# Earlier narrow rows, a new order of tap transfers and edge zeros on another engine, in a fused forward and backward kernel of an attention block

## The chip, the cores and the metric

One core of one Trainium2 chip. The metric is the device time in microseconds (us), median of several executions. A ratio of two kernels is the mean time of one kernel's fast runs over that of the other's fast runs of the same rounds, so it is not quite the ratio of the medians quoted.

PE is TensorE, DVE is VectorE, ACT is ScalarE, POOL is GpSimd, SP issues DMAs.

## The reference

```python
# B, T, D, K = 2, 4000, 144, 5; bf16
xa = layernorm(x)
q, k, v = split(xa @ w_qkv, 3)
glob = softmax(q @ k.T / sqrt(D)) @ v @ w_att_out
u, g = split(gelu(layernorm(x) @ w_mlp_in), 2)
loc  = (u * conv5(layernorm(g), dw_csgu)) @ w_mlp_out
m    = concat(glob, loc)
out  = x + (m + conv5(m, dw_merge)) @ w_merge
# returned: out, and for grad_out the gradients of
# x, w_qkv, w_att_out, w_mlp_in, dw_csgu, w_mlp_out, dw_merge, w_merge
```

## The kernel before

It does one batch after the other. Each batch has a head (transposes and projections of x and of grad_out), an attention (forward and backward, 32 blocks of rows, with the gated convolution worked off in its gaps) and a tail (gradients of the projections). D is 144, so every operand comes as 128 columns and a narrow rest of 16.

The head makes `goT`, the transposed gradient with two columns of zeros at each edge. The zeros are set by POOL. The projections of the gradient (`pb`) read this tile, the first of them with the left edge.

```python
def phase_head(k, W, b, S, nrm, ld, wts):
    ...
    goT = S.Pall[:, 2 * GW:3 * GW + 4]
    nc.gpsimd.memset(goT[:, 0:2], 0.0)
    nc.gpsimd.memset(goT[:, 2 + TT_:], 0.0)
    ...
    def stB(n, tile_q, tile_w, tile_d):
        ...
            for m in range(5):
                nc.tensor.matmul(pb[:], goT[:, i * 128 + m:i * 128 + m + 128], W.GL[...], ...)
```

The narrow rest of the keys, 16 rows, is spread by DMA to four groups of partitions, so that narrow matmuls can use it. `R_d` is a saved copy of the same rows. These DMAs go through one queue, in this order, once the head has all rows:

```python
    def spread():
        nc.sync.dma_start(S.R_d[:], R[112:128, :])
        for p in range(2):
            nc.sync.dma_start(S.Rz[p][112:128, :], ...)
        for q in range(2):
            for r in (2 * q, 2 * q + 1):
                for c0, c1, x in S.XRw:
                    nc.sync.dma_start(x[32 * r:32 * r + DR, :, 0:SC], ...)
```

The convolutions keep neighbour taps: `put` stores a block's edge rows to memory, `fill` loads the rows around a block. The tails do the same with a `fill` of their own, and POOL packs gradient taps to 80 rows (`rows80`, seen in the profile as `g<-gs`) for PE's `EF` matmuls. In the first tail POOL also computes the norm for the second batch.

Of the kernel before, what the change touches and what calls it, by code (L numbers as in the profile page):

```python
# [15 lines left out]
DR = 16  # L16
# [1043 lines left out]
TT_ = 4000  # L1060
NGR = 8
LASTR = TT_ - 31 * 128
GW_ = [512] * 7 + [416]
SC = 500
# [380 lines left out]
def phase_head(k, W, b, S, nrm, ld, wts):  # L1445

    nc, tc = k.nc, k.tc
    with ExitStack() as es:
# [4 lines left out]
        GW = NBK * 128  # L1453
        R = S.Sm[:, 2, :]
        goT = S.Pall[:, 2 * GW:3 * GW + 4]
        nc.gpsimd.memset(goT[:, 0:2], 0.0)
        nc.gpsimd.memset(goT[:, 2 + TT_:], 0.0)
        go80 = {}
        first = S.ab.tile([128, 16, 128], BF, tag="ST", bufs=3, name="go80f")
        late = S.ab.tile([128, 16, 128], BF, tag="PT", bufs=3, name="go80l")  # L1460
# [26 lines left out]
        def stT(g):  # L1487
            pm = ps_t.tile([128, 4, 128], BF, tag="tp")
            for j in range(4):
                nc.tensor.transpose(pm[:, j, :], S.xaa[:, g * 4 + j, 0:128], id_[:])  # L1490
            nc.scalar.copy(S.xaT[:, g * 512:(g + 1) * 512], pm[:].rearrange("p a b -> p (a b)"))
            pr = ps_t.tile([128, 4, 128], BF, tag="tp")
            for j in range(4):
                nc.tensor.transpose(pr[:, j, :], S.xaa[:, g * 4 + j, 16:D], id_[:])
            (nc.scalar.copy if b == 0 and g % 2 else nc.vector.tensor_copy)(R[:, g * 512:(g + 1) * 512], pr[:].rearrange("p a b -> p (a b)"))
# [30 lines left out]
                    put_dug.pop()()  # L1526

        def spread():
            nc.sync.dma_start(S.R_d[:], R[112:128, :])
            for p in range(2):  # L1530
                nc.sync.dma_start(S.Rz[p][112:128, :], R[112:128, p * 256:(p + 1) * 256])
            for q in range(2):
                for r in (2 * q, 2 * q + 1):
                    for c0, c1, x in S.XRw:
                        nc.sync.dma_start(x[32 * r:32 * r + DR, :, 0:SC], R[112:128, 0:TT_].rearrange("p (a h c) -> p a h c", h=2, c=SC)[:, c0:c1, q, :])

        def jit0():
            S.jt0 = [S.xp.tile([128, 4, 128], BF, tag=t_, name=t_) for t_ in ("QTm", "BTm", "QBr")]
# [13 lines left out]
        with tc.manual_schedule():  # L1552
            rest = None
            for g in range(3):
                if g not in S.gs:
                    take_go(k, S, b, g, ld)
            if wts:
                wts.heads(ps_t, ps_2, lambda: nrm.stats(0))
                nrm.power(0)
                wts.taps1(0)  # L1560
                wts.keys(ps_t, ps_2)
                nrm.shift(0)
                narrow(0)
                nrm.apply(0)
                wts.taps()
                wts.taps1(1)
                nrm.stats(1)
                nrm.power(1)
                stA(0)
                take_go(k, S, b, 3, ld)  # L1570
                stT(0)
                wts.rows(ps_2, 0)
                nrm.shift(1)
                nrm.apply(1)
                narrow(1)
                nrm.stats(2)
                nrm.power(2)
                wts.rows(ps_2, 1)
                rest = wts.rest(ps_t, ps_2)
            else:  # L1580
                narrow(0)
                narrow(1)
                stA(0)
                take_go(k, S, b, 3, ld)
                stT(0)
            for n in range(-1, NGR):
                if 1 <= n + 2 < NGR:
                    stT(n + 2)
                if n == 3:
                    jit0()  # L1590
                if n >= 0:
                    stB(n, *tiles())
                if 1 <= n + 2 < NGR:
                    stA(n + 2)
                if wts and n + 3 < NGR:
                    nrm.shift(n + 3)
                    nrm.apply(n + 3)
                if n + 3 < NGR:
                    narrow(n + 3)
                if wts and n + 4 < NGR:  # L1600
                    nrm.stats(n + 4)
                    nrm.power(n + 4)
                if n + 5 < NGR and n + 5 not in S.gs:
                    take_go(k, S, b, n + 5, ld)
                for f in put_dug[:len(put_dug) - n % 2]:
                    f()
                del put_dug[:len(put_dug) - n % 2]
                if n == 5:
                    spread()
                if n == 4:  # L1610
                    jit()
                if rest:
                    next(rest, None)
            for _ in rest or ():
                pass
            for f in put_dug:
                f()
            del put_dug[:]
# [153 lines left out]
def local_steps(k, W, b, S, es, ps, Q):  # L1772

    nc, tc = k.nc, k.tc
# [18 lines left out]
    def pair(p):  # L1793
        def aft(*keys):

            return tuple(((n, p - d), 0) for n, d in keys if p >= d)
# [55 lines left out]
        gn = wk.tile([128, 2, D], BF, tag="gn_t", bufs=6, name="gn_t")  # L1852
        for j in range(2):
            nc.scalar.activation(gn[:, j, :], h_[:, j, D:2 * D], ACT.Identity, bias=nm[:, j:j + 1], scale=rs[:, j:j + 1])
        yield 'P', 2, aft(("gn", 1), ("ug", 2), ("wg", 4))
        gnC.put(p, gn)
        Q.mark("gn", p)
        dug = wk.tile([128, 2, D], BF, tag="dug", name="dug")
        nc.sync.dma_start(dug[:], S.dug_d[:, 2 * p:2 * p + 2, :])
        yield 'V', 4  # L1860
        gnC.fill(p)
        yield 'P', 4, ((("gn", min(p + 1, NPR - 1)), 10),) + aft(("ug", 1))
        pc = gnC.conv(p, False)
        gc = wk.tile([128, 2, D], BF, tag="gc", bufs=1, name="gc")
# [10 lines left out]
        nc.vector.tensor_tensor(dh[:, :, 0:D], du[:], gp[:, :, 0:D], op=ALU.mult)  # L1875
        nc.sync.dma_start(S.ug_d[:, 2 * p:2 * p + 2, :], ug[:])
        Q.mark("ug", p)
        yield 'P', 1, aft(("dg", 1), ("dh", 3), ("wg", 4))
        dgC.put(p, dgc)
        Q.mark("dg", p)  # L1880
        yield 'V', 4
        dgC.fill(p)
        yield 'P', 4, ((("dg", min(p + 1, NPR - 1)), 10),) + aft(("dh", 1))
        s12 = sm.tile([128, 2, 2], F32, tag="s12", name="s12")
        dg = wk.tile([128, 2, D], BF, tag="dgf", bufs=1, name="dgf")
# [223 lines left out]
def phase_tail(k, W, b, S, nrm, nxt):  # L2109
# [3 lines left out]
    with ExitStack() as es:  # L2113
# [60 lines left out]
        def fill(g):  # L2174
            for h in range(2):
                r_ = G["r", h, g] = wk.tile([128, 512], BF, tag="r80_%d" % h, name="r80")
                taps[h].load(r_[0:80, :], g * 512, 512, nc.scalar)
# [121 lines left out]
        with tc.manual_schedule():  # L2299
            loads(0)  # L2300
            load_dh(0)
            load_dh(1)
            loads(1)
            rows80(0)
            prep(0)
            for h in range(NPR + 5):
                g, hf = divmod(h, 2)
                if 0 < h < NPR:
                    turn_dx2(*turn_dx(h))
                if hf == 0 and 0 <= g - 2 < NGR:  # L2310
                    fill(g - 2)
                if hf == 0 and g < NGR:
                    turn(g, 0)
                    corr(g, 0)
                    turn(g, 1)
                    corr(g, 1)
                elif g < NGR:
                    if g:
                        corr(g, 2)
                    corr(g, 3)  # L2320
                if h == 0:
                    turn_dx2(*turn_dx(0))
                    corr(0, 2)
                if 0 <= h - 1 < NPR:
                    sums_act(h - 1)
                    sums_dve(h - 1)
                if hf == 0 and g < NGR:
                    put(g)
                if nrm:
                    for lag, f_ in ((5, nrm.apply), (4, nrm.shift), (3, nrm.power), (2, nrm.stats), (1, nrm.load)):  # L2330
                        q, m = divmod(h - lag, 2)
                        if m == 0 and 0 <= q < NGR:
                            f_(q)
                    if NPR + 2 <= h < NPR + 4:
                        narrow_go(k, nxt, h - NPR - 2, nrm.ld)
                if h == NPR - 1:
                    spill_ef()
                if fin_ and 4 <= h < NPR - 1:
                    fin_.loads(h - 4)
                if g + 1 < NGR:  # L2340
                    (rows80 if hf else prep)(g + 1)
                if 0 <= h - 1 < NPR:
                    means(h - 1)
                if 0 <= h - 2 < NPR:
                    fin(h - 2)
                if h == NPR + 4:
                    spill_gr()
                if 0 <= h - 5 < NPR:
                    out_mm(h - 5)
                if fin_ and h == NPR + 4:  # L2350
                    fin_.gr_out()
                if NPR <= h < NPR + 4:
                    for q in range(4):
                        j = (h - NPR) * 8 + 2 * q
                        gr_part(range(j, j + 2))
                        if fin_:
                            fin_.step((h - NPR) * 4 + q)
                if h < NPR:
                    dx_mm(h)
                if hf == 0 and 0 <= g - 1 < NGR:  # L2360
                    load_x(g - 1)
                if nrm and NPR - 2 <= h < NPR + 1:
                    take_go(k, nxt, 1, h - NPR + 2, nrm.ld)
                if hf == 1 and g + 2 < NGR:
                    load_dh(g + 2)
                    loads(g + 2)
# [346 lines left out]
```

## Time and profile before

| | before |
|---|---|
| time, median of 3 (lowest to highest) | 1281.05 us (1277.03 to 1282.44) |
| span of the profiled run, mean granted clock | 1278.3 us, 0.993 |
| PE busy | 1210.3 us, 95% |
| first head, attention, tail | 53.1, 497.0, 89.7 us |
| second head, attention, tail | 30.9, 496.7, 110.9 us |

A stage is measured by marks on PE: an attention begins with the first 128-row matmul of scores (`pS<-..,QTm`), a tail with its first transpose `pt<-w_ident,Q_t`, the second head with its first transpose `tp<-w_ident,gs`. These are the stages of every table below.

Busy time by microsecond in the second head, the columns after the length being PE, PEld, DVE, ACT and POOL busy, then granted clock, DMA share and GB/s:

```profile
644.00:645.00 1.00, 0.00 (x0) 0.00 (x0) 0.00 (x0) 0.00 (x0) 0.04 (x1) 1.00 1.15 352
645.00:646.00 1.00, 0.10 (x1) 0.10 (x2) 0.00 (x0) 0.00 (x0) 1.00 (x6) 0.61 1.06 363
646.00:647.00 1.00, 1.00 (x5) 0.64 (x6) 0.00 (x0) 0.00 (x0) 0.46 (x2) 0.50 0.45 151
651.00:652.00 1.00, 1.00 (x7) 0.65 (x5) 0.14 (x1) 0.40 (x1) 0.00 (x0) 0.50 1.02 372
652.00:653.00 1.00, 1.00 (x10) 0.78 (x9) 0.31 (x1) 0.23 (x1) 0.00 (x0) 0.98 0.67 245
```

In 644 to 645 PE does nothing. The clock falls inside the next microsecond (0.61 is a mean of 1.00 and 0.50, so it fell at about 645.2) and returns at about 652.0. PE was idle from 643.25 to 645.90. The timeline of PE in the first head, and the waits from 655 us on, which hold the second attention (total, times, longest):

```profile
51.18 0.37 PE L1982 MATMUL pS<-rb,QBr 16*128 16x500 bf16 x1 [0.21 <-DMA rb<-Sm]
```

```profile
PE pD L1982 <- DVE Sm L1996: 2.4, 11, 0.4
```

The first is the smaller of two waits for the narrow rows in the first head (the larger, 1.26 us, is in the prediction), 1.47 us together. The second line is PE's usual wait for DVE in an attention, eleven short ones, 2.4 us in all.

### The profile page before, as it was taken

Reading aid. Unit: us, or ns where it says so; the run is one execution under the profiler, and the core shown is the slowest. Engines: PE = TensorE matmul, PEld = TensorE weight load, DVE = VectorE, ACT = ScalarE, POOL = GpSimd, SP = SyncE. Lnnn points to the kernel's source line nnn. Section 1 sums busy time; section 2 is a strip of 40 time slices with the busy share of each in tenths; the row PEclk is TensorE's granted clock in tenths of the full one; section 3 lists DMA queues with packets and bytes.
Section 4 is the critical chain, followed back from the end, with each engine's and each line's share of the span. In section 5 each row is a group of like instructions: output and inputs, shape, how many; then the busy total and the mean of one; then the engine's idle time right before and its main releaser. Section 6 shows DMA issues by size and latency. Waiting matters only on the chain.

```text
span 1278.3 us, 39805 instructions
## 1 busy us (share of the span) xinstructions
PE 1210.3 (95%) x15118; PEld 949.6 (74%) x15118; DVE 959.7 (75%) x3257; ACT 842.4 (66%) x2494; POOL 556.2 (44%) x1011
## 2 busy tenths in 40 slices
PE   7899999999999999989989999999999999998996
PEld 4667777777777777789865777777777777778984
DVE  7567788889788887857536677888888878885674
ACT  5777777776777666556557777776776776654542
POOL 6323454544445532357512244454544445325650
PEclk9999999999999999999989999999999999999998
DMA  7379888998998999977746998999889998998861
GB/s 207 96 137 173 154 158 153 162 157 153 166 156 153 164 159 161 160 216 217 201 146 124 160 153 149 154 169 170 151 158 156 154 166 154 163 154 204 235 171 31
DMA packets 633616, 205.43 MB, mean 161 GB/s; under 512 B 576719, under 2 KB 630948, under 8 KB 633380
## 3 DMA queue, kind: packets, MB, share of 16 engines
q1 hardware_dynamic: 626912, 197.46, 81.6%
q10 hardware_dynamic: 6500, 5.32, 1.7%
q8 instruction: 120, 1.97, 0.6%
q14 instruction: 84, 0.69, 0.2%
HBM read 46.11 MB, written 21.79 MB: 53 GB/s over the span
## 4 chain that ended last, share of the span: by engine, by line
PE 66%; DVE 14%; DMA 7%; ACT 5%; issue 4%; POOL 2%; SPq 1%; ACTq 0%; DVEq 0%; POOLq 0%
PE y L2032 15%; PE pS L1986 9%; PE X L2054 8%; PE X L2055 8%; PE pD L1986 7%; PE pS L1982 5%; DVE Sm L1996 5%; PE pc L1692 2%; PE pb L1518 2%; DVE jg L1913 2%; DMA gs<-in_grad_out_dram 1%; PE gr L2286 1%; DMA y<-r 1%; DMA f_EF<-EF_d 1%; DVE acc L2070 1%
## 5 line engine op out<-in xcount | busy, mean ns | idle before, releaser
L1996 DVE SCALAR_TENSOR_TENSOR Sm<-pD,Pm 128x500 bf16<-128x500 f32 x512 | 325.7, 673 | 80.1 <-PE pD L1986 46.0
L1994 ACT ACTIVATE Pm<-pS 128x500 bf16<-128x500 f32 x512 | 295.4, 586 | 43.7 <-PE pS L1986 40.9
L2054 PE MATMUL X<-Qs,Sm 128*128 128x144 bf16 x2048 | 285.6, 226 | 9.3 <-DVE acc L2070 8.9
L2067 POOL TENSOR_TENSOR acc<-xs,acc 128x432 f32<-128x432 f32 x150 | 168.0, 1120 | 280.8 <-ACT xs L2066 280.3
L2055 PE MATMUL X<-Bt,Pm 128*128 128x144 bf16 x2048 | 285.4, 226 | 0.7 <-DVE Bt L2019 0.7
L2055 PEld LDWEIGHTS <-Pm 128*128 128x128 bf16 x2048 | 200.2, 98 | 11.9 <-issue 11.3
L2054 PEld LDWEIGHTS <-Sm 128*128 128x128 bf16 x2048 | 200.1, 98 | 1.5 <-issue 0.9
L2032 PEld LDWEIGHTS <-PT 128*128 128x128 bf16 x2048 | 136.6, 98 | 31.3 <-issue 3.2
L2032 PEld LDWEIGHTS <-ST 128*128 128x128 bf16 x2048 | 136.4, 98 | 27.5
L2066 ACT COPY xs<-X 128x432 f32<-128x432 f32 x150 | 77.9, 519 | 111.3 <-PE X L2055 103.0
L2070 DVE TENSOR_TENSOR acc<-X,acc 128x432 f32<-128x432 f32 x180 | 104.0, 578 | 52.9 <-PE X L2055 52.3
L1994 ACT ACTIVATION_READ_ACCUMULATOR Pm<-pS 128x1 f32 x512 | 104.8, 205 | 0.0
L1982 PE MATMUL pD<-rb,QBr 16*128 16x500 bf16 x448 | 95.5, 378 | 3.5 <-DVE Sm L1996 3.0
L1982 PE MATMUL pS<-rb,QBr 16*128 16x500 bf16 x448 | 91.8, 379 | 3.1 <-DMA rb<-Sm 2.8
L1986 PEld LDWEIGHTS <-BTm 128*128 128x128 bf16 x512 | 49.8, 98 | 59.9 <-issue 1.6
L1913 DVE SCALAR_TENSOR_TENSOR jg<-gnC,dgC 128x256 bf16<-128x256 bf16 x160 | 91.7, 573 | 1.0
L1986 PEld LDWEIGHTS <-QTm 128*128 128x128 bf16 x512 | 29.0, 97 | 75.5 <-issue 75.5
L2042 POOL TENSOR_TENSOR B_t<-zd,yd 128x144 bf16<-128x144 f32 x64 | 33.7, 526 | 112.6 <-ACT zd L2041 112.2
L1986 PE MATMUL pS<-rb,QTm 128*128 128x500 bf16 x256 | 76.5, 380 | 0.0
L1986 PE MATMUL pS<-ra,QTm 128*128 128x500 bf16 x256 | 76.5, 380 | 0.0
L2032 PE MATMUL y<-ra,PT 128*128 128x144 bf16 x1024 | 74.3, 226 | 1.6 <-ACT zd L2041 1.6
L2032 PE MATMUL y<-rb,PT 128*128 128x144 bf16 x1024 | 74.3, 226 | 1.3 <-ACT zd L2041 1.3
(638 smaller groups left out, 2877.8 us busy)
## 6 DMA issues: line engine op xcount, KB each, us to landing
gs<-in_grad_out_dram SPq DMA_DIRECT2D x24, 720.0 KB
dh_d<-dh SPq DMA_DIRECT2D x32, 144.0 KB
dhr<-dh_d SPq DMA_DIRECT2D x16, 288.0 KB
gs<-in_grad_out_dram SPq DMA_DIRECT2D x8, 540.0 KB
xg<-in_x_dram SPq DMA_DIRECT2D x21, 144.0 KB
dug_d<-dug SPq DMA_DIRECT2D x16, 144.0 KB
dug<-dug_d SPq DMA_DIRECT2D x32, 72.0 KB
ug_d<-ug SPq DMA_DIRECT2D x32, 72.0 KB
```

The lines of the kernel that those rows point to most:

```text
L1913: nc.vector.scalar_tensor_tensor(jg[:], a_[:, m:m + 256], 1.0, d_[:, 2:258], op0=ALU.mult, op1=ALU.mult, accum_out=dws[:, p, m:m + 1])
L1982: nc.tensor.matmul(o_[h][:, 0:SC], jt[i // 4][2][rr, i % 4, :], S.XR[c2][rr, 0:SC], start=True, stop=False)
L1986: nc.tensor.matmul(o_[h][:, 0:SC], jt[i // 4][w][:, i % 4, :], S.xaT[:, c0:c0 + SC], start=False, stop=True)
L1994: nc.scalar.activation(P[:, pb, c1:c1 + SC], o_[h][:, 0:SC], ACT.Exp, accum_out=ld8[:, 0, n_:n_ + 1])
L1996: nc.vector.scalar_tensor_tensor(Sm[:, pb, c1:c1 + SC], o_[h][:, 0:SC], 1.0, P[:, pb, c1:c1 + SC], op0=ALU.mult, op1=ALU.mult, accum_out=l ...
L2032: nc.tensor.matmul(y[:, w, :], src[:, jj, :], S.xaa[:, j, :], start=(j == 0), stop=(j == NBK - 1))
L2042: nc.gpsimd.tensor_tensor(S.Zn[:, i, :], zd[:], yd[:], op=ALU.add)
L2054: nc.tensor.matmul(X[:, jj, :], Sm[:, i % NP, j * 128:(j + 1) * 128], Qs[:, i % 4, :], start=(kk == 0 and jj == 0), stop=False, skip_group ...
L2055: nc.tensor.matmul(X[:, jj, :], P[:, i % NP, j * 128:(j + 1) * 128], Bt[:, i % 4, :], start=False, stop=(kk == 1), skip_group_check=True)
L2066: nc.scalar.copy(xs[:, 0:nj, :], X[:, 0:nj, :])
L2067: nc.gpsimd.tensor_tensor(a_, xs[:, 0:nj, :], a_, op=ALU.add)
L2070: nc.vector.tensor_tensor(a_, X[:, 0:nj, :], a_, op=ALU.add)
```

## The change

Its intent: the zeros should not stand behind a packing on POOL that waits for a load, the narrow rows should be on their way before the copy that nobody awaits, and transfers of taps should be ordered so that the queue does not wait for itself.

```diff
@@ phase_head
-        nc.gpsimd.memset(goT[:, 0:2], 0.0)
-        nc.gpsimd.memset(goT[:, 2 + TT_:], 0.0)
+        nc.vector.memset(goT[:, 0:2], 0.0)
+        nc.vector.memset(goT[:, 2 + TT_:], 0.0)
@@ spread
+            for c0, c1, x in S.XRw:
+                for q in range(2):
+                    for r in (2 * q, 2 * q + 1):
+                        nc.sync.dma_start(x[32 * r:32 * r + DR, ...], ...)
+                if c0 == 0:
+                    for p in range(2):
+                        nc.sync.dma_start(S.Rz[p][112:128, :], ...)
             nc.sync.dma_start(S.R_d[:], R[112:128, :])
-            (the Rz and x DMAs of before, which followed R_d)
@@ head loop: the call moves from after the projections of step 5 to before them
+                if n == 5:
+                    spread()
@@ gated convolution in the attention (and the same with "dg" and "df")
-        yield 'P', 2, aft(("gn", 1), ("ug", 2), ("wg", 4))
+        yield 'P', 2, aft(("gn", 1), ("gf", 1), ("ug", 2), ("wg", 4))
         gnC.put(p, gn)
 ...
         gnC.fill(p)
+        Q.mark("gf", p)
@@ tail loop
-                if hf == 0 and 0 <= g - 2 < NGR:
+                if hf == 0 and 0 <= g - 2 < NGR - 1:
                     fill(g - 2)
+                if h == NPR + 1:
+                    fill(NGR - 1)
 ...
+                if hf == 1 and g + 1 < NGR:
+                    rows80(g + 1)            # now ahead of the norm on POOL
 ...
-                if g + 1 < NGR:
-                    (rows80 if hf else prep)(g + 1)
+                if hf == 0 and g + 1 < NGR:
+                    prep(g + 1)
```

## The prediction

> **What bounds the kernel now.** I read the page first (busy shares and the row of the granted clock), then busy time by stage, then the list of waits inside the stages the change touches, and last the timelines of PE, POOL and SP around each wait on that list. The program does two batches one after the other; each has a head (projections), an attention loop and a tail. First the page, then the three stages that carry the argument: first attention, first tail, second head.

> ```profile
> PE 1210.3 (95%) x15118; PEld 949.6 (74%) x15118; DVE 959.7 (75%) x3257; ACT 842.4 (66%) x2494; POOL 556.2 (44%) x1011
> ...
> PEclk9999999999999999999989999999999999999998
> ...
> 54.00:545.00 491.00, 477.83 (x5817) 361.40 (x5816) 392.88 (x1275) 344.83 (x1044) 208.71 (x356) 1.00 0.91 156
> ...
> 562.00:645.00 83.00, 74.45 (x1166) 71.93 (x1163) 55.60 (x225) 48.35 (x126) 47.42 (x91) 1.00 0.75 207
> 645.00:671.00 26.00, 23.58 (x228) 18.98 (x229) 9.92 (x31) 13.54 (x37) 4.03 (x13) 0.87 0.42 126
> ```

> In a stage line the first figures after the length are PE's busy time, then PEld, DVE, ACT, POOL, and the clock is the third number from the end. PE is busy 477.8 of 491 us in an attention: it is the bound there, and nothing in the change takes PE work away. So the change can earn only what PE waits elsewhere, at most 1278 - 1210 = 68 us, plus the time PE runs slow. The slice with clock 8 is the second head (mean 0.87). The waits of tail and second head, in total, times, longest:

> ```profile
> PE EF L2190 <- POOL g L2152: 5.0, 4, 2.5
> PE pb L1518 <- POOL Pm L1456: 2.7, 1, 2.7
> PE pS L1982 <- DMA rb<-Sm: 1.3, 1, 1.3
> ```

> These are three of the changed lines: the 80-row packing of the gradient taps, the edge zeros and the narrow rows. The second head, first on POOL, then on PE:

> ```profile
> 644.96 0.46 POOL L1437 TENSOR_SCALAR g<-gs 128x320 bf16<-128x320 bf16 x1 [6.33 <-DMA gs<-in_grad_out_dram]
> ...
> 645.75 0.10 POOL L1456 MEMSET Pm<- 128x2 bf16 x1
> ...
> 643.02 0.23 PE L1511 MATMUL pq<-w_M,Sm 128*128 128x144 bf16 x1
> 645.90 1.38 PE L1518 MATMUL pb<-w_GL,Pm 128*128 128x288 bf16 x5 [2.66 <-POOL Pm L1456]
> ...
> 652.23 0.78 PE L1518 MATMUL pb<-w_GL,Pm 128*128 128x288 bf16 x5
> ...
> 645.90:652.04 6.14, 6.13 (x37) 4.74 (x38) 1.46 (x4) 2.03 (x5) 1.02 (x4) 0.50 0.33 113
> ```

> [...]The edge memset of 0.10 us stands behind a packing that waits 6.33 us for a gradient load, and PE waits 2.66 us for the memset. Then the same five matmuls take 1.38 us at 645.90 and 0.78 us at 652.23: for 6.14 us PE ran at clock 0.50. The memset thus costs twice, by the wait and by the slow clock after it.

> [...]clock by the microsecond puts the slow stretch from about 645.2 to 652.0[...]the chain has the third narrow-row DMA of the second head landing 2.17 us after its issue begins.[...]

> **The change part by part.** The changed kernel, built but not run, has the same work on every engine; only order and engine differ, and few places differ at all.

> 1. Edge zeros by VectorE. In the second head the two memsets now stand on DVE directly behind the last output addition of the tail (ends 640.4), with no wait of their own. PE's operands are otherwise there: its last matmul before the wait begins at 643.02, and the rows it needs were copied by 643.0. So PE goes on near 643.2 and saves 2.66 us.[...] 6.14 us at half rate becomes 3.07, saving 3.07. Sum 5.7 us. The next gradient load landed at 644.8, and the transposes that need it come about 647.3 in the new order, so it does not take the place of the wait. In the first head the memsets at 1.3 us gate nothing: 0.

> 2. Narrow rows. The queue now issues what the first attention matmuls read first; the saved copy of all rows goes last. Second head, SP and then PE:

> ```profile
> 663.55 0.32 SPq L1529 DMA_DIRECT2D R_d<-Sm  x1
> 663.92 1.53 SPq L1531 DMA_DIRECT2D Rz<-Sm  x2
> 665.49 0.65 SPq L1535 DMA_DIRECT2D rb<-Sm  x1
> ...
> 668.63 0.38 PE L1982 MATMUL pS<-rb,QBr 16*128 16x500 bf16 x1
> 670.35 0.37 PE L1982 MATMUL pS<-rb,QBr 16*128 16x500 bf16 x1 [1.35 <-DMA rb<-Sm]
> ```

> The third rb DMA is the one awaited; it starts at 668.14. In the new order it starts 2 x 0.69 us after 663.55, at 664.93, and lands near 667.1, before PE asks (668.7). PE's next matmuls move from 670.65 to about 668.95: 1.7 us saved. In the first head the same reordering brings the first rb issue from 47.95 to 46.28, but here the built PE stream differs: the first of the two narrow matmuls has been placed two projections earlier, ahead of work that starts at 47.60. It now waits for a DMA[...]. So PE stalls 0.9 to 1.6 us earlier instead of

> ```profile
> 52.81 0.37 PE L1982 MATMUL pS<-rb,QBr 16*128 16x500 bf16 x1 [1.26 <-DMA rb<-Sm]
> ```

> and then has 3.2 us of projections before the second. The matmuls that followed at 53.10 come at 52.3 to 53.0: about 0.5 us saved, not the 1.5 that the order on the queue alone would give.

> 3. Packing ahead of the norm on POOL, first tail only (the second has no norm beside it). Of POOL's order before

> ```profile
> 566.23 0.19 POOL L1413 TENSOR_SCALAR ve<-mv 128x4 f32<-128x4 f32 x1
> 566.50 1.02 POOL L1414 TENSOR_TENSOR rstdx<-ve,w_mhalf 128x4 f32<-128x4 f32 x1
> 567.62 0.46 POOL L2152 TENSOR_SCALAR g<-gs 128x320 bf16<-128x320 bf16 x1
> ```

> the packing moves up by 567.62 - 566.23 = 1.39 us. PE's four waits for it are 0.89 (the first group, which is not moved), 2.5, 0.84 and 0.77. At most 1.39 + 0.84 + 0.77 = 3.0 us; but at the 0.84 wait the next transposes were held by ACT to within 0.4 us of the same time, and DVE is busy 3.7 of 4 us around the 2.5. I take 2.0.

> 4. Taps. In both attentions the store of the last taps stood ahead of a load of earlier ones, and the load waited for it:

> ```profile
> SPq L1646 <- DMA dgC_d<-dgC0s: 2.7, 1, 2.7
> ```

> That wait goes, and the transposes behind it on SP start up to 2.5 us sooner. But PE never waited for them here: its waits at that end are 1.64 us for ACT, held by the conv gradient's buffer, and under 0.4 for others. The last loads now stand behind another transpose, which can eat their slack. I count 0, give or take 0.5 us each.

> 5. Last taps of a tail read sooner: PE's only wait for taps in the first tail, 1.5 us, is for group 6, which is not moved; for group 7 there is none, nor in the second tail. I count 0.

> Sum: 5.7 + 1.7 + 0.5 + 2.0 = 9.9 us. Attention is bound by PE and only follows, so all of it should reach the end: 1281 - 10 = 1271 us, 0.8% less.

> **The rivals.** First, the clock falls anyway:[...] the start of the second head has small gaps between 640.6 and 641.9. For it speaks that 2.66 us of idle were enough; against it, that the 2.4 us idle at 565 to 568 left the clock at 1.00. Then 3 us less is won: 1274. Second, a wait takes the place of the removed ones: the gradient load in the second head, or the narrow matmul placed early in the first head, if its DMA lands behind the weight stores issued just before. That would cost 1 to 2 us of the sum; the DMA engines were idle from 44 to 47 us, which speaks against it. Third, the first tail is bound by DVE and ACT as much as by PE's waits, and part 3 gives nothing: 1273. Fourth, upward: the tap queue did hold the end of the attentions (the chain of waits passes through the store, 4 us each), and the freed queue gives 1 to 2 us each: 1268.

> **Range and chances.** The three runs of before spread over 5 us, the rivals over 1268 to 1276. I say 1271, 80% between 1266 and 1276. Faster by 2% would need 26 us, more than all parts at their highest; slower by 2% would need a new stall of 26 us. So faster 0.02, within 2% 0.97, slower 0.01.

> **What would show it.** Second head: first edge matmul near 2.7 us after the last projection no more but at once, clock 1.00 throughout, five matmuls at 0.78 us from the start; stage shorter by about 7 us. The second narrow matmul without a wait there, and in the first head a wait of about 1 us two projections earlier. First tail: packing waits near 1 us in sum in place of 4.1 for the moved groups, the stage about 2 us shorter. Both attentions within 1 us of 491. I am wrong if the clock in the second head still falls, if an attention changes by more than 1.5 us, or if the first tail does not get shorter.

## The result, and the profile after

| | before | after |
|---|---|---|
| median (lowest to highest), runs | 1279.91 us (1277.03 to 1282.44), 4 | 1273.02 us (1271.15 to 1274.07), 4 |
| ratio, 95% interval | | 0.9945, 0.9919 to 0.9972 |
| profiled span, clock | 1278.3 us, 0.993 | 1269.4 us, 0.997 |
| first head | 53.10 | 50.11 |
| first attention | 496.99 | 497.74 |
| first tail | 89.68 | 89.95 |
| second head | 30.88 | 23.29 |
| second attention | 496.73 | 497.61 |
| second tail | 110.92 | 110.70 |

By ratio the time fell 0.55%, 7.0 us; the median lies in the predicted range and the class is "within 2%". But the stages add differently from the sum that was predicted. The page of the changed kernel, its busy time and its clock:

```profile
PE 1206.0 (95%) x15118; PEld 946.8 (75%) x15118; DVE 962.5 (76%) x3261; ACT 843.4 (66%) x2494; POOL 558.3 (44%) x1007
...
PEclk9999999999999999999999999999999999999998
```

The "8" in the middle of the clock row is gone (the last one is the end of the program). The second head by stage, before and then after, with the same columns as above:

```profile
639.77:670.65 30.88, 26.46 (x273) 21.40 (x271) 12.58 (x38) 16.62 (x43) 4.07 (x13) 0.89 0.49 150
```

```profile
637.80:661.09 23.29, 22.96 (x273) 19.49 (x271) 12.56 (x40) 16.16 (x42) 3.88 (x11) 1.00 0.68 202
```

PE does the same 273 recorded matmuls; its busy time falls from 26.46 to 22.96 us, and that is the clock (mean 0.89 and 1.00). The rest of the 7.6 us is idle time, 4.42 us before and 0.33 after. The reasons, from DVE's timeline and PE's:

```profile
638.41 0.06 DVE L1456 MEMSET Pm<- 128x1 uint32 x1
```

```profile
640.96 0.23 PE L1511 MATMUL pq<-w_M,Sm 128*128 128x144 bf16 x1
641.02 0.78 PE L1518 MATMUL pb<-w_GL,Pm 128*128 128x288 bf16 x5
...
660.78 0.38 PE L1985 MATMUL pS<-rb,QBr 16*128 16x500 bf16 x2
```

DVE sets the first edge zeros at 638.41, PE needs them at 641.02 and goes straight on from the projections at 640.96, and the two narrow matmuls at 660.78 no longer wait. The first head, PE and then SP:

```profile
46.17 0.38 PE L1985 MATMUL pS<-rb,QBr 16*128 16x500 bf16 x1
...
50.11 0.60 PE L1989 MATMUL pS<-rb,QTm 128*128 128x500 bf16 x2
```

```profile
41.61 4.57 SPq L1532 DMA_DIRECT2D rb<-Sm  x4
```

The narrow matmul that the new order puts early runs at 46.17 with no wait, because the queue issues the first rows from 41.61 on. They need only the groups of rows that are there by then, as an exchange of the two halves bears out below. The prediction had this matmul stall for 0.9 to 1.6 us. The first tail, PE's waits:

```profile
PE po L2219 <- DMA r<-u: 1.8, 1, 1.8
PE EF L2193 <- POOL g L2155: 1.7, 2, 0.9
PE EF L2193 <- DMA ug<-ug_d: 1.6, 2, 1.2
PE pt L2169 <- ACT hT L2209: 0.8, 2, 0.6
```

The waits for POOL's packing fell, 5.0 us in four to 1.7 in two, but waits for a load of `ug` (in this one of the five profiles with the new packing alone) and for ACT's `hT` are new, and the stage is no shorter. The wait for DVE in the second attention:

```profile
PE pD L1985 <- DVE Sm L1999: 2.9, 12, 0.5
```

One wait more, of 0.5 us. That is the opposite of what the new order of the taps was for.

### The profile page after: what moved, and what is told of

It is laid out like the page before.

```text
span 1269.4 us, 39810 instructions
## 1 busy us (share of the span) xinstructions
PE 1206.0 (95%) x15118; PEld 946.8 (75%) x15118; DVE 962.5 (76%) x3261; ACT 843.4 (66%) x2494; POOL 558.3 (44%) x1007
## 4 chain that ended last, share of the span: by engine, by line
PE 71%; DVE 13%; DMA 4%; ACT 4%; issue 4%; POOL 1%; SPq 0%; ACTq 0%; DVEq 0%; POOLq 0%
PE y L2035 15%; PE pS L1989 9%; PE X L2057 8%; PE X L2058 8%; PE pD L1989 7%; DVE Sm L1999 5%; PE pS L1985 5%; PE pb L1518 3%; PE pc L1693 2%; PE EF L2193 2%; PE po L2218 2%; DVE jg L1916 2%; DMA ug<-ug_d 1%; PE gr L2289 1%; DVE acc L2073 1%
## 5 line engine op out<-in xcount | busy, mean ns | idle before, releaser
L2035 PEld LDWEIGHTS <-ST 128*128 128x128 bf16 x2048 | 136.4, 98 | 27.6
```

The source lines that it names most:

```text
L2035: nc.tensor.matmul(y[:, w, :], src[:, jj, :], S.xaa[:, j, :], start=(j == 0), stop=(j == NBK - 1))
```

## The experiments

Twelve runs: eight kernels with one part alone or one part undone (one of them with added work), then four repetitions. Each was profiled once; the stages are in the table that follows the last of them.

**The zeros alone.** Only the two memsets move to DVE.

```diff
-        nc.gpsimd.memset(goT[:, 0:2], 0.0)
-        nc.gpsimd.memset(goT[:, 2 + TT_:], 0.0)
+        nc.vector.memset(goT[:, 0:2], 0.0)
+        nc.vector.memset(goT[:, 2 + TT_:], 0.0)
```

> The kernel before, with only the edge zeros moved to VectorE. Theory (the zeros cost twice, by PE's wait and by the slow clock after it): second head 5.5 to 6.0 us shorter (30.9 to about 25.1 from its first gradient transpose to the first full attention matmul), granted clock 1.00 through it, span 5 to 6 us shorter. Rival (the clock falls at that point anyway): 2.6 us shorter, clock 0.50 for some 6 us still.

Measured: second head 24.84 us against 30.88, clock 1.00 all through it, ratio 0.9972 (0.9948 to 0.9995). The step of 6.0 us agrees with the predicted 5.7, and the rival that the clock falls anyway finds no support, here or in the other four profiles with the zeros on DVE. The time gained only 3.6 us, though, which was the first sign that one profile is not the kernel.

**The rows alone, whole and in two versions.** First the whole part, then only the new order of the queue with the call left in its place, and with the two halves exchanged (`q` 1 first), so that the first DMA has to wait for the last rows.

```diff
# rows_only: new spread(), and the call moved ahead of the projections of step 5
# rows_swap: new spread() with the halves exchanged, call not moved
-                for q in range(2):
+                for q in (1, 0):
```

> The kernel before, with only the narrow rows' DMAs moved and reordered. Theory (the first two row DMAs read only the first seven eighths of the narrow rows, so with nothing ahead of them on the queue they go before the last eighth is there): first head 3.0 us shorter as in the whole change, second head 1.7 us shorter, span 4.5 to 5 us shorter. Rival (the first head's 3.0 us came from another part of the change): first head 0.5 us shorter, span 2 us shorter.

> The kernel before, with the narrow rows' DMAs ahead of the saved copy, but the two DMAs that need the last eighth of the rows put first. If the theory of rows_only is right, the queue now stands until the rows are complete, at 46.3 us, and the first full attention matmul of the first head comes near 51.5 instead of 53.1 (1.6 us saved, not 3.0); second head 1.7 us shorter as there. Rival (what matters is only that the saved copy no longer stands ahead): the same 3.0 us as rows_only in the first head.

Measured: first head 49.51 and 51.31 us, second head 27.83 and 27.75, ratios 0.9984 (0.9952 to 1.0016) and 0.9962 (0.9934 to 0.9991). In the exchanged version the queue and PE of the first head, SP and then PE:

```profile
46.23 2.68 SPq L1532 DMA_DIRECT2D rb<-Sm  x4
```

```profile
51.00 0.39 PE L1983 MATMUL pS<-rb,QBr 16*128 16x500 bf16 x2
```

The rows are issued 4.6 us later than in the changed kernel (up to 1.7 us of it is a slow stretch at 20.5 us, explained below), there is no early narrow matmul, and still neither of the two narrow matmuls shows a wait. So what the first head gains is the waits of before (1.47 us in the first profile, 0.70 to 1.49 us in the eight without this part, none in the six with it), and comes from the order on the queue; the earlier issue adds nothing that can be seen here. The 1.8 us between the two first heads is not from the rows at all, as the last section of the experiments shows: both first heads came close to what the two theories expected, and that was luck, for a slow stretch lay in one and none in the other. A kernel with the earlier call alone, in the old order, came out with the same instructions in the same order as before on every engine, so it was not run.

**Everything but the tap order.** The changed kernel without the two new conditions.

```diff
-        yield 'P', 2, aft(("gn", 1), ("gf", 1), ("ug", 2), ("wg", 4))
+        yield 'P', 2, aft(("gn", 1), ("ug", 2), ("wg", 4))
-        yield 'P', 1, aft(("dg", 1), ("df", 1), ("dh", 3), ("wg", 4))
+        yield 'P', 1, aft(("dg", 1), ("dh", 3), ("wg", 4))
```

> The changed kernel without its two new waits of the tap stores. Theory (these waits move the last transposes of each attention one place later on PE, and with them VectorE's order, so that each attention got 0.8 us longer): both attentions 0.7 to 0.9 us shorter than in the changed kernel, span 1.5 us shorter than its 1269.4. Rival (the 0.8 us come from the attentions starting earlier against the DMAs, or from scatter): attentions as long as in the changed kernel, within 0.2 us.

Measured: second attention 496.89 us, as expected; first attention 498.65, against the expectation; ratio 0.9934 (0.9910 to 0.9959).

**The tap order alone.** The same two lines, added to before.

> Before with the new order of the tap stores alone. Theory (the transposes of the last taps come one place later on PE, VectorE's product queues behind an accumulation that waits for PE, and PE waits 0.50 us for Sm at the end): both attentions 0.7 to 0.9 us longer than 497.0, with a PE wait of 0.50 us for Sm in each. Rival (scatter or another part of the change made the attentions of the changed kernel longer): both within 0.3 us of 497.0. Rest as in before; ratio about 1.001.

Measured: attentions 497.51 and 497.27 us, ratio 1.0002 (0.9983 to 1.0020). PE's waits in the second attention have the longer line:

```profile
PE pD L1984 <- DVE Sm L1998: 2.9, 12, 0.5
```

This is 2.4 to 2.9 us and eleven to twelve waits, as in the changed kernel. The mechanism holds, but the size is 0.5 us an attention and not the 0.7 to 0.9 expected.

**The packing alone.**

```diff
+                if hf == 1 and g + 1 < NGR:
+                    rows80(g + 1)
                 if 0 <= h - 1 < NPR:
                     sums_act(h - 1)
 ...
-                    (rows80 if hf else prep)(g + 1)
+                    prep(g + 1)              # under hf == 0
```

> Before with the 80-row packing moved ahead of the norm on POOL in the first tail, nothing else. The prediction: PE's waits for POOL's packing fall from 5.0 us in four to about 1.7 in two and the first tail is 2.0 us shorter (89.7 to 87.7). Rival: the packing waits fall just so, but waits for other things (the load of ug, ACT's hT, DVE's t) appear in their place, and the first tail is within 1 us of 89.7. Second head still 30.9 with the slow clock, attentions within 0.3 us of 497 in both.

Measured: first tail 90.59 us, ratio 0.9996 (0.9979 to 1.0013). PE's waits:

```profile
PE EF L2190 <- POOL g L2152: 1.9, 2, 1.0
PE pt L2166 <- ACT hT L2206: 1.1, 1, 1.1
```

The packing waits fell as predicted and ACT's `hT` took their place: the rival. The two expectations on the attentions and the second head failed, in a telling way: the first attention was 498.68 us and the second head 27.73, where nothing was changed in either.

**The last fill alone.**

```diff
-                if hf == 0 and 0 <= g - 2 < NGR:
+                if hf == 0 and 0 <= g - 2 < NGR - 1:
                     fill(g - 2)
+                if h == NPR + 1:
+                    fill(NGR - 1)
```

> Before with only the last fill of each tail read sooner. Theory: nothing waits for that group, both tails within the scatter of the earlier runs (88 to 90 and 110.6 to 113.4 us), no wait of PE for those taps in either kernel, ratio 1.000 within 0.002. Rival: the earlier read delays a transfer that something waits for, and the load waits of the tails (r from u 1.5 us, ug) grow by 0.5 us or more.

Measured: tails 89.04 and 112.94 us, ratio 0.9998 (0.9967 to 1.0029). Nothing was gained or lost beyond the scatter. The longest load wait of the second tail for `ug` was 1.5 us here against 0.5 in before, but 1.3 in the run of the packing alone, which does not have the earlier fill, so it need not be this part's.

**The clock without the change.** Before, with 44 idle transposes on PE ahead of the edge matmuls, into a tile that nobody reads. The wait for the memset stays; PE is busy in it.

```diff
+            if b == 1 and n == 0:
+                warm = ps_t.tile([128, 4, 128], BF, tag="tp", name="warm")
+                for _ in range(44):
+                    nc.tensor.transpose(warm[:, 0, :], S.xaa[:, 0, 0:128], id_[:])
```

> Before with nothing of the change; only 44 idle transposes added on PE, into a spare tile nobody reads, between the last projection of the second head and the edge matmuls. The memset stays on POOL, so the wait of 2.66 us stays, but PE is busy in it. Theory (the idle time trips the clock): clock 1.00 through the second head, the five edge matmuls take 0.78 us and not 1.38, the second head is about 3.1 us shorter (30.9 to about 27.8) with the edge matmuls starting no sooner; ratio about 0.9976. Rival (the clock falls there for another reason): clock 0.50 for about 6 us all the same, the second head within 0.3 us of 30.9 or longer by the added work.

Measured, PE's timeline and then one microsecond:

```profile
645.12 2.62 PE L1515 MATMUL warm<-w_ident,rb 128*128 128x128 bf16 x44
648.03 0.79 PE L1522 MATMUL pb<-w_GL,Pm 128*128 128x288 bf16 x5 [0.29 <-POOL Pm L1456]
```

```profile
647.00:648.00 1.00, 0.74 (x14) 0.56 (x11) 0.00 (x0) 0.00 (x0) 0.93 (x5) 1.00 1.02 356
```

The memset is still awaited, 0.29 us after the fillers; the five matmuls take 0.79 us, the clock is 1.00 and the second head 27.74 us, as expected. Alone this does not show that the idle time trips the clock. The ratio was 1.0006 (0.9984 to 1.0028), not 0.9976, and the kernels with the packing alone and the tap order alone had second heads of 27.73 and 27.63 us with the full wait of 2.6 us and no fillers. Their clock did not fall there either. The kernel with the packing alone, second head:

```profile
644.00:645.00 1.00, 0.00 (x0) 0.00 (x0) 0.01 (x1) 0.25 (x1) 0.00 (x0) 1.00 1.12 351
645.00:646.00 1.00, 0.00 (x0) 0.00 (x0) 0.00 (x0) 0.00 (x0) 0.59 (x2) 1.00 1.07 378
646.00:647.00 1.00, 0.64 (x6) 0.52 (x7) 0.00 (x0) 0.00 (x0) 0.92 (x6) 1.00 0.97 328
```

PE is idle for two whole microseconds and parts of two more, 2.56 us in all and nearly as long as in before, and the clock stays at 1.00.

**What differs between executions.** This needed a search of all profiles for microseconds with a clock under 1.00. The exchanged-rows run has four, each the beginning of a slow stretch of 3.4 us:

```profile
20.00:21.00 1.00, 0.33 (x4) 0.20 (x4) 0.97 (x7) 0.58 (x1) 0.72 (x3) 0.76 1.05 397
78.00:79.00 1.00, 0.80 (x3) 0.15 (x2) 1.00 (x4) 0.36 (x2) 0.00 (x0) 0.78 0.38 114
645.00:646.00 1.00, 1.00 (x7) 0.69 (x6) 0.31 (x1) 0.28 (x1) 0.24 (x1) 0.58 0.00 0
1174.00:1175.00 1.00, 1.00 (x14) 1.00 (x12) 0.00 (x0) 0.00 (x0) 0.92 (x3) 0.62 0.62 171
```

From the means the clock fell at 20.52, 78.56, 645.16 and 1174.24 us. The distances are 17.00, 166.00 and 155.01 times 3.4133 us. The first profile of before gives the length of one stretch itself: its trace records the clock at 0.50 for 3.413 us from 20.58 us on, and for 6.827 us, two such lengths, from 645.22 us on; the two beginnings are 183.00 times 3.4133 us apart. In the second profile of the changed kernel, quoted below, the falls at 21.28, 79.30 and 690.30 us are 17.00 and 179.00 times 3.4133 us apart. Counted in steps of 3.4133 us from the start of the span, the falls do not come at the same places: in the second head the remainder is 0.10 us in the first profile of before (645.22) and 0.79 us in the third (645.91). At clock 0.50 a stretch of 3.41 us should cost half its length, 1.7 us, where PE is the bound; this is an estimate from the two figures, and the table below bears it out: second heads of the old zeros and rows took 27.6 to 27.7 us with no stretch, 29.3 with one and 30.9 with two. Four repetitions tested this: before twice, the changed kernel, and the changed kernel without the tap order.

> The kernel before once more, unchanged, for another profile. Theory [...]: the wait of 2.6 us for the memset is there again, the fixed work of the second head takes 27.6 us within 0.3 after taking off 1.7 us for each slow stretch of 3.4 us in it, and the number of such stretches need not be two as in the first profile of the same kernel. Rival (the slow clock belongs to the program): two stretches again, second head 30.9 us, one stretch near 20 us in the first head, none elsewhere before the end.

> The same kernel a third time, same expectations as the one ahead: by the theory the number of slow stretches in the second head may be 0, 1 or 2, and all stretches of one execution lie whole multiples of 3.413 us apart; by the rival two again at the same places.

> The changed kernel again. Theory: no idle in the second head, so no slow stretch there[...], and the second head 23.3 us within 0.1; slow stretches may appear now near 20 us, in 76 to 82 us or in the first tail, 1.7 us each, which its first profile did not have. First head 49.5 to 50.2 us without and 51.2 to 51.9 with a stretch; attentions 497.4 to 497.8 less the stretches. Time about 0.9945 of before. Rival: it again has none, and its span is 1269.4 within 0.5.

> The changed kernel without the new order of the tap stores, again. Theory: attentions 496.7 to 497.1 us after taking off slow stretches, so 0.5 to 0.9 us less in each than the changed kernel, 1.0 to 1.8 us in all, about 0.9990 of the changed kernel's time (0.9935 against 0.9945 of before). Rival: the attentions of the two agree within 0.2 us and so do their times within the interval.

Measured: the same kernel before now had one stretch in the second head in both profiles, not two; a second one lay in the first tail in one of them and in the first head in the other. Third profile of before, second head:

```profile
646.00:647.00 1.00, 0.97 (x5) 0.62 (x6) 0.00 (x0) 0.00 (x0) 0.59 (x3) 0.50 0.58 194
649.00:650.00 1.00, 1.00 (x18) 1.00 (x17) 0.60 (x2) 0.53 (x2) 0.00 (x0) 0.88 0.00 0
```

Here the clock is back in 649 to 650, where the first profile still had 0.50 at 651 to 652. The changed kernel's second profile had none in the second head (23.31 us), and three others, one of them where no earlier profile had any:

```profile
690.00:691.00 1.00, 0.85 (x3) 0.20 (x3) 0.97 (x5) 0.80 (x2) 0.00 (x0) 0.65 0.97 129
```

Its first profile, with none, had been the lucky one of the two. The times: the changed kernel 1274.34 us (1273.39 to 1275.00, 6 runs), 0.9965 of before (0.9949 to 0.9981); without the tap order 1271.87 us (1270.20 to 1273.33, 6 runs), 0.9945 (0.9928 to 0.9962); before 1278.21 us (1275.13 to 1282.12, 11 runs).

All stages as measured, in us, an asterisk for each slow stretch in it; the last column is the span less 1.71 us for each:

| run | head | attention | tail | head | attention | tail | span | less stretches |
|---|---|---|---|---|---|---|---|---|
| before | 53.10* | 496.99 | 89.68 | 30.88** | 496.73 | 110.92 | 1278.3 | 1273.2 |
| before_a | 51.43 | 497.05 | 89.59* | 29.30* | 496.78 | 111.75 | 1275.9 | 1272.5 |
| before_b | 53.48* | 496.84 | 89.59 | 29.34* | 496.57 | 112.98 | 1278.8 | 1275.4 |
| fill_only | 52.25 | 496.99 | 89.04 | 29.26* | 496.72 | 112.94 | 1277.2 | 1275.5 |
| pack_only | 51.05 | 498.68* | 90.59* | 27.73 | 497.00 | 113.15 | 1278.2 | 1274.8 |
| taps_only | 51.90* | 497.51 | 91.34* | 27.63 | 497.27 | 111.95 | 1277.6 | 1274.2 |
| warm | 52.70* | 497.05 | 92.06** | 27.74 | 498.00 | 110.55 | 1278.1 | 1273.0 |
| zeros_only | 52.81* | 497.13 | 88.48 | 24.84 | 497.01 | 110.63 | 1270.9 | 1269.2 |
| rows_only | 49.51 | 498.49* | 89.12 | 27.83* | 496.80 | 112.45 | 1274.2 | 1270.8 |
| rows_swap | 51.31* | 498.37* | 88.60 | 27.75* | 496.53 | 113.44* | 1276.0 | 1269.2 |
| after | 50.11 | 497.74 | 89.95 | 23.29 | 497.61 | 110.70 | 1269.4 | 1269.4 |
| after_again | 51.79* | 499.28* | 88.45 | 23.31 | 498.84* | 111.53 | 1273.2 | 1268.1 |
| after_free_taps | 51.59* | 498.65* | 88.05 | 23.29 | 496.89 | 112.03 | 1270.5 | 1267.1 |
| free_taps_again | 51.51* | 498.72* | 88.62 | 23.29 | 498.49* | 110.77 | 1271.4 | 1266.3 |

With 1.71 us taken off for each asterisk the stages of like kernels agree. The second head is 27.5 to 27.7 us with the old zeros and old rows (seven runs), 26.0 and 26.1 with the new rows, 24.8 with the new zeros, 23.3 with both (four runs). The unexpected 498.7 of a first attention is 497.0. In the table only the second attention of the run with fillers, 498.00 us, stays unexplained by this.

## Why the prediction was right or wrong

**The time was right, and the sum behind it was not.** 1271 us with 1266 to 1276 held both measured medians, 1273.0 and 1274.3. Its sum was 9.9 us; the ratios give 7.0 and 4.5. The terms, each as the difference of group means of the table with the stretches taken off:

| term | predicted | measured |
|---|---|---|
| zeros: PE's wait, second head | -2.66 | -2.8 |
| zeros: slow clock, second head | -3.07 | -1.5, mean of eight executions |
| rows, second head | -1.7 | -1.5 |
| rows, first head | -0.5 | -1.4 (six runs with, eight without) |
| packing, first tail | -2.0 | -0.2 (five with, nine without) |
| tap order, both attentions | 0 | +1.1 (three with, eleven without) |
| last fill, first and second tail | 0 | -0.1 and -0.2, inside the scatter |
| sum without the last fill | -9.9 | about -6.3 |

The slow clock is counted for the second head alone. Stretches elsewhere did not become fewer: over the whole program the three profiles of before had 3, 2 and 2, the changed kernel 0 and 3, and the changed kernel without the tap order 2 and 3. So part of the 1.5 us may not reach the time; these few profiles can't tell how much.

**Edge zeros.** The mechanism was right in both halves: DVE's zeros need no wait, no other wait took the place, and the clock stays up (1.00 over the second head of the changed kernel). The step that failed is the size of the slow clock, "6.14 us at half rate becomes 3.07, saving 3.07". It took what one profile showed as what the kernel costs. Eight profiled executions had the memset wait unfilled: the three of before, and those with the rows (two), the fill, the packing and the tap order alone. Their second heads had 2, 1, 1, 1, 1, 1, 0 and 0 stretches. Seven times 1.71 us over eight is 1.5 us. The prediction had the slow stretch of one profile, from about 645.2 to 652.0, and did not ask whether another execution of the same kernel would show it as long. The same holds for its argument against the clock falling anyway, that 2.4 us of idle at 565 us had left the clock alone. There the idle time came to 1.11 and 1.42 us in two steps of 3.4133 us; in the second profile of before 2.03 us of the same wait fell into one step, and the clock fell at 566 us.

**Narrow rows.** Right in the second head. In the first head the step that failed is "It now waits for a DMA", and with it "So PE stalls 0.9 to 1.6 us earlier". The DMA was taken to need all rows, as its place in the queue before suggested. It needs only some, and with the saved copy behind it the queue issues it from 41.61 us. The "1.5 that the order on the queue alone would give" is what came: 1.47 us of waits went, and the stage is 1.4 us shorter. The trace has the awaited DMA landing 2.17 us after its issue began in the second head and 2.38 in the first. The length of the stall was an estimate: an issue at 46.28 us and 2.17 us give 48.45, 0.9 us after 47.60; no figure gives the 1.6.

**Packing.** The step "I take 2.0" failed, and the third rival was right. The waits did fall, from 3.3 to 5.0 us in the runs without to 1.7 to 2.0 in the five with, but the waits for ACT (`pt` from `hT`, 0.8 to 1.2 us) and for DVE (`t`, 0.6 to 0.7) that came up in their place fit the same work finishing at the same time; no run isolates this. The prediction named "if the first tail does not get shorter" as a sign that it is wrong, and for this part it is. It had seen that ACT held the next transposes and counted it as a deduction of one part in three; it was nearly all.

**Taps.** "I count 0, give or take 0.5 us each" was at the edge: 0.66 and 0.45 us in the means, in the wrong direction, and 0.5 us of it is the one longer wait for DVE. The argument that PE never waited for those taps held. What it left out is that the later place of the transposes also moves DVE's work. The product on DVE then queues behind an accumulation that waits for PE itself, so the tile `Sm` comes 0.5 us late. The chain for this was read in the timeline of the changed kernel; that the tap order alone brings the wait, and that taking it out removes it, is shown by the runs.

**What the first profile seemed to say.** Spans fell 8.9 us, and 3 times 1.7 of that was the clock, of which the changed kernel's execution had none. That the spans fell by nearly the predicted sum was in part chance.

The best version is the changed kernel without the tap order: 0.9934 and 0.9945 of before, against 0.9945 and 0.9965 for the changed kernel. In the rounds they shared, 1271.87 against 1274.34 us, and no run of the first was above the lowest of the second.

**What stays open.** In the first head (at about 20.5 us) and early in both attentions (78.6, and 690) the clock fell in some executions with little idle time in the step of 3.4133 us before: 0.80 to 1.06 us at nine falls in first heads, 0.36 to 0.50 us at eight in the attentions. So idle time alone does not order the falls there: in the tails and second heads steps of up to 1.82 us were followed by none. In the step before the fall in the first attention of the run with the packing alone, narrow matmuls run one after another on 16 of 128 rows:

```profile
77.31 0.38 PE L1982 MATMUL pS<-rb,QBr 16*128 16x500 bf16 x1
77.77 0.37 PE L1982 MATMUL pD<-rb,QBr 16*128 16x500 bf16 x1
77.83 0.37 PE L1982 MATMUL pS<-rb,QBr 16*128 16x500 bf16 x1
```

The first profile of before has the same three at 79.36, 79.82 and 79.88 us, and its clock did not fall in that attention. No run was made to test what the falls there come from, and it stays open.

## What to carry to other kernels

Before a slow stretch is counted as a cost of a wait, profile the same kernel two or three times: here a wait of 2.6 us cost 0, 1.7 or 3.4 us more in slow clock, with the same instructions. Compare kernels by stages with the slow stretches taken off, and leave to the timed rounds what the clock adds on average. And when a wait at an engine is shortened, ask first what else arrives at the same time: over 2 us of packing waits went, and the stage stayed as long as it was.
